# Loading the output weights in 4 KB rows, with selection matmuls, and in DMAs over uneven groups of partitions

## Chip, cores, metric

One core of one Trainium2 chip. The metric is the device time of one execution in microseconds (us); every kernel was run several times and compared with runs of the kernel before on the same chip. Names used below: PE is the matmul engine, PEld its weight loads, DVE, ACT and POOL the vector, scalar and general-purpose engines, and SP the one that issues the large loads; SBUF is the core's memory of 128 partitions, PSUM the one that matmuls write, HBM the chip's main memory. A packet is one entry in the trace's list of what the DMA engines moved, and a load has landed when the last of its completions is in the trace. The profile's span is 1 to 3 us shorter than the device time of the same kernel.

## The reference, cut to what matters

```python
B, Sq, D = 32, 1, 512
Hq, Hkv, Sk, Dh = 32, 8, 2048, 128          # all bfloat16
W = 512                                     # the last 512 rows of the caches are used
q = (x @ wq) -> [B, Hq, 1, Dh]
p = softmax(q . k[:, :, -W:] * Dh**-0.5)    # k, v: [B, Hkv, Sk, Dh], each shared by 4 heads
o = p . v[:, :, -W:]                        # [B, Hq, 1, Dh]
out = o.reshape(B, Sq, Hq*Dh) @ wo          # wo: [4096, 512], 4.19 MB
```

The 512 rows of K and V for 32 batches and 8 heads are 67 MB of the 75.5 MB that are read from HBM, so this is a kernel that streams: its time goes into moving bytes (403 to 411 GB/s while K and V come in).

## The kernel before

One queue (SP) issues every large load: wq, then K and V for the 32 batches, then wo into the place of wq. K and V rows are 4 KB each, 128 partitions a DMA, 512 KB a DMA. wo comes last, in four DMAs whose pieces are 1 KB (one row of wo, 512 numbers): partition d gets row `h*128 + d` for each head h.

```python
WO_CUT = (0, 10, 20, 28, 32)
...
w_sb = sb("w_sb", [P, DKT * HD], BF16)
wo_sb = w_sb[:, :].rearrange("p (h n) -> p h n", h=HQ)
oT_sb = sb("oT_sb", [P, B, HQ], BF16)
...                                          # SP queue, after all K and V issues
sp.wait_ge(pe_qt, 1)
for c in range(4):
    h0, h1 = WO_CUT[c], WO_CUT[c + 1]
    sp.dma_start(
        wo_sb[:, h0:h1, :],
        wo[h0 * DH:h1 * DH, :].rearrange("(h d) n -> d h n", d=P),
    ).then_inc(sem_wo[c], 16)
...                                          # PE, after the last P.V
for hq in range(HQ):
    if hq in WO_CUT:
        pe.wait_ge(sem_wo[WO_CUT.index(hq)], 16)
    for c in range(4):
        ins = pe.matmul(
            KT_ps[:, 0, :].bitcast(F32)[32 * c:32 * (c + 1), 0:128],
            lhsT=oT_sb[:, :, hq], rhs=wo_sb[:, hq, c * 128:(c + 1) * 128],
            start=(hq == 0), stop=(hq == HQ - 1), tile_position=(0, 32 * c),
        )
```

## Time and profile before

| | before |
|---|---|
| time, median of 4 | 198.11 us (197.87 to 198.22) |
| span of the profiled run | 196.5 us |
| last wo part landed | 192.91 us |
| rate while K and V stream | 403 to 411 GB/s |
| rate from 182 to 188 us (wo) | 340 GB/s |
| mean time of a wo packet (1 KB), 182 to 188 us | 50 ns |

From the page of the kernel before: the row of DMA busy tenths and the row of GB/s (40 slices of the span each), the packet line, the chain that ended last (by engine, then by line: L128 issues K, L136 V, L148 wo), the wo matmuls, and the wo issues (size of one, and median us from issue to landing).

```profile
DMA  5999999999999999999999999999999999999970
GB/s 205 425 417 409 411 405 409 411 409 405 409 409 405 408 407 409 410 407 410 404 409 408 409 409 404 410 406 409 406 408 408 408 409 403 409 404 350 338 253 16
DMA packets 23374, 75.95 MB, mean 386 GB/s; under 512 B 2325, under 2 KB 6453, under 8 KB 22837
...
SPq 52%; DMA 37%; PE 7%; issue 2%; DVE 0%
DMA K_sb<-in_k_cache_dram 32%; SPq L136 25%; SPq L128 18%; SPq L148 8%; DMA w_sb<-in_wo_dram 5%; PE KT_ps L229 4%; PE QO_ps L279 1%; PE S_ps L246 1%; SPq L122 1%; PE KT_ps L301 0%; SPq L110 0%; DVE out_sb L368 0%
...
L301 PE MATMUL KT_ps<-w_sb,oT_sb 128*32 128x128 bf16 x128 | 4.3, 313 | 6.6 <-DMA w_sb<-in_wo_dram 6.6
...
w_sb<-in_wo_dram SPq DMA_DIRECT2D x2, 1280.0 KB, 19.3
w_sb<-in_wo_dram SPq DMA_DIRECT2D x1, 1024.0 KB, 12.7
w_sb<-in_wo_dram SPq DMA_DIRECT2D x1, 512.0 KB, 9.9
```

The engines are busy almost everywhere and the chain is DMA and the issuing of DMAs for 89% of the span: nearly all of its time goes into moving bytes, at 403 to 411 GB/s while K and V stream. Only the last four slices fall, 350, 338, 253, 16 GB/s: that is wo.

The table of stretches shows the same end more finely. Its columns are the stretch, its length, the busy us (and instructions) of PE, weight load, DVE, ACT and POOL, then the granted clock, the DMA share and GB/s.

```profile
core 0: us, PE busy (x) PEld busy (x) DVE busy (x) ACT busy (x) POOL busy (x), PEclk, DMA share, GB/s
170.00:176.00 6.00, 2.65 (x48) 2.50 (x48) 3.64 (x7) 1.32 (x3) 0.00 (x0) 0.66 1.03 406
176.00:182.00 6.00, 3.52 (x109) 3.10 (x108) 0.57 (x3) 1.36 (x2) 0.00 (x0) 0.50 1.02 356
182.00:188.00 6.00, 2.02 (x68) 1.70 (x64) 0.19 (x1) 0.00 (x0) 0.00 (x0) 0.50 1.05 340
188.00:194.00 6.00, 3.02 (x88) 2.27 (x88) 0.29 (x1) 0.00 (x0) 0.00 (x0) 0.50 0.42 140
```

One more reading comes from the semaphore events in the trace. A 128-partition DMA gives sixteen completions in the trace; I read them as one from each of the sixteen DMA engines, which the trace doesn't number. These are the completions of the last wo part of the kernel before, in us, sorted:

```
189.31 189.33 189.38 189.46 189.86 189.89 190.04 190.25 190.83 190.96 191.32 192.25 192.32 192.35 192.56 192.91
```

Some engines end 3.6 us behind others. At 14 us the spread was 0.7 us. It grows in steps of about 1.55 us of one completion at a time, each step beside one of the 21 packets of 16 KB in the queue that the page calls "instruction" (about 1.08 us each). Over the K loads the spread jumps at the first, ninth and seventeenth of these (15.05, 85.38 and 152.98 us): from 0.7 to 1.9, from 2.3 to 3.5 and from 3.9 to 5.0 us, so the steps go round eight of the sixteen. In the K load that begins to land at 149.4 us, eight completions lie 3.2 to 3.9 us behind the first and the others at most 1.2 us.

### The profile page before, as it was taken

How to read it: one execution, taken by the hardware profiler on the slowest of the kernel's cores; microseconds unless marked ns; L12 is line 12 of the kernel's file. 1: busy time of each engine (PE TensorE's matmuls, PEld its weight loads, DVE VectorE, ACT ScalarE, POOL GpSimd, SP SyncE). 2: the span in 40 equal slices, each digit the busy share in tenths (PEclk: the TensorE clock that was granted, in tenths of full speed). 3: DMA queues.
4: the chain of work that ended last, by engine and by line, in shares of the span. 5: the costliest groups of instructions: out<-in, count | busy, mean ns of one | idle time of the engine just before them, and what ended most of it. 6: DMA issues, size and time to landing. Idle time of an engine off the chain costs nothing.

```text
span 196.5 us, 6073 instructions
## 1 busy us (share of the span) xinstructions
PE 142.8 (73%) x2692; PEld 116.4 (59%) x2692; DVE 99.8 (51%) x187; ACT 56.5 (29%) x67; POOL 12.1 (6%) x43
## 2 busy tenths in 40 slices
PE   0448994987787797749786979779997599746423
PEld 0337773875575576637665858656975477535322
DVE  0006789645774479424952695457645647541000
ACT  3002434433262145203342325232432052320000
POOL 8102000000000010000000000000000000000000
PEclk9999999699999799985999797996699759955555
DMA  5999999999999999999999999999999999999970
GB/s 205 425 417 409 411 405 409 411 409 405 409 409 405 408 407 409 410 407 410 404 409 408 409 409 404 410 406 409 406 408 408 408 409 403 409 404 350 338 253 16
DMA packets 23374, 75.95 MB, mean 386 GB/s; under 512 B 2325, under 2 KB 6453, under 8 KB 22837
## 3 DMA queue, kind: packets, MB, share of 16 engines
q1 hardware_dynamic: 23300, 75.54, 97.5%
q8 instruction: 21, 0.34, 0.7%
q10 hardware_dynamic: 48, 0.03, 0.2%
q14 instruction: 5, 0.03, 0.0%
HBM read 75.53 MB, written 0.03 MB: 384 GB/s over the span
## 4 chain that ended last, share of the span: by engine, by line
SPq 52%; DMA 37%; PE 7%; issue 2%; DVE 0%
DMA K_sb<-in_k_cache_dram 32%; SPq L136 25%; SPq L128 18%; SPq L148 8%; DMA w_sb<-in_wo_dram 5%; PE KT_ps L229 4%; PE QO_ps L279 1%; PE S_ps L246 1%; SPq L122 1%; PE KT_ps L301 0%; SPq L110 0%; DVE out_sb L368 0%
## 5 line engine op out<-in xcount | busy, mean ns | idle before, releaser
L229 PE MATMUL KT_ps<-perm,K_sb 128*128 128x128 bf16 x1024 | 76.0, 238 | 20.7 <-DMA K_sb<-in_k_cache_dram 20.5
L324 DVE COPY KT_sb<-KT_ps 128x1024 bf16<-128x1024 bf16 x96 | 63.3, 687 | 54.0 <-PE KT_ps L229 53.7
L229 PEld LDWEIGHTS KT_ps<-perm,K_sb 128*128 128x128 bf16 x1024 | 67.5, 108 | 27.1 <-DMA K_sb<-in_k_cache_dram 26.0
L383 ACT ACTIVATE KT_sb<-KT_ps 128x1024 bf16<-128x1024 bf16 x32 | 32.7, 1023 | 81.8 <-PE KT_ps L229 81.8
L279 PEld LDWEIGHTS QO_ps<-PT_sb,V_sb 128*128 128x128 bf16 x1024 | 28.2, 98 | 17.4 <-issue 12.7
L279 PE MATMUL QO_ps<-PT_sb,V_sb 128*128 128x16 bf16 x1024 | 31.1, 171 | 3.7 <-DMA V_sb<-in_v_cache_dram 1.9
L346 DVE TENSOR_SCALAR P_ex<-P_f,recip 32x512 bf16<-32x512 f32 x32 | 25.3, 792 | 1.1
L246 PE MATMUL S_ps<-KT_sb,QBD 128*32 128x512 bf16 x256 | 21.4, 414 | 0.0
L401 ACT ACTIVATE PT_sb<-PT_ps 128x1024 bf16<-128x1024 bf16 x16 | 15.5, 1020 | 20.4 <-PE PT_ps L261 20.4
L261 PE MATMUL PT_ps<-ident,P_ex 128*128 128x128 bf16 x128 | 11.8, 266 | 9.6 <-DVE P_ex L346 9.6
L261 PEld LDWEIGHTS PT_ps<-ident,P_ex 128*128 128x128 bf16 x128 | 10.1, 122 | 10.7 <-DVE P_ex L346 10.7
L189 POOL COPY QBD<-QT_sb 128x32 bf16<-128x32 bf16 x32 | 7.4, 245 | 117.9 <-PE S_ps L246 108.0
L353 DVE CAST oT_sb<-QO_ps 128x32 bf16<-128x32 f32 x32 | 5.9, 183 | 8.9 <-PE QO_ps L279 8.8
L301 PE MATMUL KT_ps<-w_sb,oT_sb 128*32 128x128 bf16 x128 | 4.3, 313 | 6.6 <-DMA w_sb<-in_wo_dram 6.6
L207 PE MATMUL PT_ps<-xT_sb,w_sb 128*128 128x32 bf16 x128 | 4.1, 188 | 6.2 <-DMA w_sb<-in_wq_dram 6.2
L301 PEld LDWEIGHTS KT_ps<-w_sb,oT_sb 128*32 128x32 bf16 x128 | 3.3, 158 | 7.4 <-DMA w_sb<-in_wo_dram 4.7
L207 PEld LDWEIGHTS PT_ps<-xT_sb,w_sb 128*128 128x128 bf16 x128 | 3.7, 104 | 6.6 <-DMA w_sb<-in_wq_dram 4.6
L330 DVE TENSOR_REDUCE maxv<-S_ps 128x1 f32<-128x512 f32 x8 | 5.5, 691 | 4.0 <-PE S_ps L246 4.0
L391 ACT ACTIVATE P_f<-S_ps,negmax 128x512 f32<-128x512 f32 x8 | 5.5, 687 | 5.4 <-DVE negmax L332 5.4
L246 PEld LDWEIGHTS S_ps<-KT_sb,QBD 128*32 128x32 bf16 x256 | 3.9, 96 | 3.7 <-issue 1.0
L316 DVE CAST QT_sb<-PT_ps 128x512 bf16<-128x512 f32 x1 | 0.7, 691 | 10.0 <-PE PT_ps L207 10.0
L368 DVE CAST out_sb<-KT_ps 128x128 bf16<-128x128 f32 x1 | 0.3, 292 | 10.7 <-PE KT_ps L301 10.7
(20 smaller groups left out, 11.9 us busy)
## 6 DMA issues: line engine op xcount, KB each, us to landing
K_sb<-in_k_cache_dram SPq DMA_DIRECT2D x64, 512.0 KB, 15.6
V_sb<-in_v_cache_dram SPq DMA_DIRECT2D x64, 512.0 KB, 15.4
w_sb<-in_wq_dram SPq DMA_DIRECT2D x4, 1024.0 KB, 8.4
w_sb<-in_wo_dram SPq DMA_DIRECT2D x2, 1280.0 KB, 19.3
w_sb<-in_wo_dram SPq DMA_DIRECT2D x1, 1024.0 KB, 12.7
w_sb<-in_wo_dram SPq DMA_DIRECT2D x1, 512.0 KB, 9.9
x_sb<-in_x_dram ACTq DMA_DIRECT2D x1, 32.0 KB, 3.2
out_dram<-out_sb SPq DMA_DIRECT2D x1, 32.0 KB
```

Of the source, the lines that this page charges most:

```text
L128: sp.dma_start(K_sb[:, b % NK, h].rearrange("p r d -> p (r d)"), cache_rows(k_cache, b, h)).then_inc(sem_k[b % NK][h], 16)
L136: sp.dma_start(V_sb[:, b % NV, h].rearrange("p r d -> p (r d)"), cache_rows(v_cache, b, h)).then_inc(sem_v[b % NV], 16)
L148: sp.dma_start(wo_sb[:, h0:h1, :], wo[h0 * DH:h1 * DH, :].rearrange("(h d) n -> d h n", d=P),).then_inc(sem_wo[c], 16)
L207: ins = pe.matmul(PT_ps[:, h // 16, :].bitcast(F32)[:, (h % 16) * 32:(h % 16 + 1) * 32], lhsT=wq_sb[:, kt, h * DH:(h + 1) * DH], rhs=xT_sb ...
L229: ins = pe.matmul(KT_ps[:, t, i * 128:(i + 1) * 128], lhsT=K_sb[:, b % NK, h, 8 * (t % 2) + i, :], rhs=perm[:, :, :], start=True, stop=Tru ...
L246: ins = pe.matmul(S_ps[32 * c:32 * c + 32, :], lhsT=QBD[:, b % NQB, g, :], rhs=KT_sb[:, b % NKT, h, :, c, :], start=(j == 0 and h == 0), s ...
L261: ins = pe.matmul(PT_ps[:, r // 8, (r % 8) * 128:(r % 8 + 1) * 128], lhsT=P_ex[:, r, :, :].rearrange("p s g -> p (s g)"), rhs=ident[:, :], ...
L279: ins = pe.matmul(QO_ps[:, 16 * h:16 * h + 16], lhsT=V_sb[:, b % NV, h, r, :], rhs=PT_sb[:, q % 2, r, :].rearrange("p (c n) -> p c n", c=G ...
L324: dve.tensor_copy(KT_sb[:, b % NKT, t // 2, 8 * (t % 2):8 * (t % 2) + 8, :, :], KT_ps[:, t, :]).then_inc(dve_T, 1)
L346: dve.tensor_scalar(P_ex[rows, :, :, c], P_f32[rows, :].rearrange("p (r s) -> p r s", r=NR), recip[rows, q:q + 1], None, op0=ALU.mult,).th ...
L383: act.activation(KT_sb[:, b % NKT, 1, 8:16, :, :], KT_ps[:, 3, :], ACTF.Copy).then_inc(act_T, 1)
L401: act.activation(PT_sb[:, q % 2, 8 * i:8 * i + 8, :].rearrange("p r n -> p (r n)"), PT_ps[:, i, :], ACTF.Copy,).then_inc(act_PT, 1)
```

## The change

The intent is to shorten the wo phase twice: by 4 KB pieces, and by levelling the sixteen DMA engines. Partition p now gets four neighbouring rows of wo (4 KB in one piece), so the attention output has to be regrouped to match: "selection" matmuls with a band of ones move element d of head h to partition `(h%4)*32 + d//4`, index `d%4`. wo is cut into eight parts of 512 KB, and five of these are issued as DMAs over uneven groups of partitions, which take different numbers of engines.

```diff
-    WO_CUT = (0, 10, 20, 28, 32)
+    NHG = HQ // 4
+    SELCUT = 28
+    WO_SPLIT = [(128,), (4, 4, 120), (56, 72), (40, 88), (2, 6, 120), (24, 104), (128,), (128,)]
@@ SP queue
-            for c in range(4):
-                ...
+            for hg in range(NHG):
+                p0 = 0
+                for m in WO_SPLIT[hg]:
+                    sp.dma_start(
+                        wo_sb[p0:p0 + m, hg].rearrange("p i n -> p (i n)"),
+                        wo[hg * 512 + 4 * p0:hg * 512 + 4 * (p0 + m), :].rearrange("(m i) n -> m (i n)", i=4),
+                    ).then_inc(sem_wo[hg], 16)
+                    p0 += m
@@ PE
+            def select(b0, b1, dst):
+                pe.wait_ge(dve_oT, b1)
+                for i in range(4):
+                    for hi in range(4):
+                        ins = pe.matmul(
+                            dst(i), lhsT=band[:, i, 96 - 32 * hi:224 - 32 * hi],
+                            rhs=oT_sb[:, :, b0:b1].rearrange("p (g hi) b -> p hi g b", hi=4)[:, hi],
+                            start=(hi == 0), stop=(hi == 3), ...)
+                ins.then_inc(pe_sel, 1)
+  ... select(0, 28, ...) after batch 28 of P.V, select(28, 32, ...) at the end
+            for hg in range(NHG):
+                pe.wait_ge(sem_wo[hg], 16 * len(WO_SPLIT[hg]))
+                for i in range(4):
+                    for c in range(4):
+                        ins = pe.matmul(..., lhsT=o_sel[:, i, hg, :], rhs=wo_sb[:, hg, i, c * 128:(c + 1) * 128], ...)
```

Also: DVE and ACT copy the selected output from PSUM, the final result is copied in four pieces by these two engines, and it is stored in 1 KB rows instead of 256 B ones.

More of the change, by code (lines that the diff above doesn't have):

```diff
@@ L52, in bass_standalone__sliding_block_cached__sampling_kernel @@
         wq_sb = w_sb[:, :].rearrange("p (kt n) -> p kt n", kt=DKT)
-        wo_sb = w_sb[:, :].rearrange("p (h n) -> p h n", h=HQ)
+        wo_sb = w_sb[:, :].rearrange("p (g i n) -> p g i n", g=NHG, i=4)
         K_sb = sb("K_sb", [P, NK, 2, NR, DH], BF16)
@@ L61, in bass_standalone__sliding_block_cached__sampling_kernel @@
         PT_sb = sb("PT_sb", [P, 2, NR, P], BF16)
-        oT_sb = sb("oT_sb", [P, B, HQ], BF16)
+        oT_sb = sb("oT_sb", [P, HQ, B], BF16)
+        o_sel = sb("o_sel", [P, 4, NHG, B], BF16)
+        band = sb("band", [P, 4, 224], BF16)
         xT_sb = sb("xT_sb", [P, DKT, 32], BF16)
@@ L66, in bass_standalone__sliding_block_cached__sampling_kernel @@
         x_sb = sb("x_sb", [32, D], BF16)
-        out_sb = sb("out_sb", [P, 128], BF16)
+        out_sb = sb("out_sb", [32, 4, 128], BF16)
         maxv = sb("maxv", [P, NQUAD], F32)
@@ L80, in bass_standalone__sliding_block_cached__sampling_kernel @@
         sem_wq = [sem(f"sem_wq{i}") for i in range(DKT)]
-        sem_wo = [sem(f"sem_wo{i}") for i in range(4)]
+        sem_wo = [sem(f"sem_wo{i}") for i in range(NHG)]
         sem_k = [[sem(f"sem_k{i}_{h}") for h in range(2)] for i in range(NK)]
@@ L91, in bass_standalone__sliding_block_cached__sampling_kernel @@
         pe_fin = sem("pe_fin")
+        pe_sel = sem("pe_sel")
+        dve_sel = sem("dve_sel")
+        act_sel = sem("act_sel")
+        act_out = sem("act_out")
+        pool_band = sem("pool_band")
         pool_perm = sem("pool_perm")
@@ L145, in _ @@
             sp.wait_ge(pe_qt, 1)
-            for c in range(4):
-                h0, h1 = WO_CUT[c], WO_CUT[c + 1]
-                sp.dma_start(
-                    wo_sb[:, h0:h1, :],
-                    wo[h0 * DH:h1 * DH, :].rearrange("(h d) n -> d h n", d=P),
-                ).then_inc(sem_wo[c], 16)
-            sp.wait_ge(dve_out, 1)
+            for hg in range(NHG):
[6 more added lines that the diff above has]
+                    p0 += m
+            sp.wait_ge(dve_out, 2)
+            sp.wait_ge(act_out, 2)
             sp.dma_start(
-                out.rearrange("b s (c n) -> c (b s) n", c=4), out_sb[:, :]
+                out.rearrange("b s n -> b (s n)"), out_sb[:, :, :].rearrange("b c n -> b (c n)")
             ).then_inc(sem_out, 16)
@@ L174, in _ @@
             pool.memset(P_ex[:, :, :, :], 0.0).then_inc(pool_ex, 1)
+            pool.memset(band[:, :, :], 0.0).then_inc(pool_band, 1)
+            pool.wait_ge(pool_band, 1)
+            pool.affine_select(
+                out=band[:, :, :], in_=band[:, :, :], compare_op=ALU.not_equal, fill=1.0,
+                base=384, pattern=[[-1, 4], [-4, 224]], channel_multiplier=1,
+            ).then_inc(pool_band, 1)
             pool.wait_ge(pool_init, 4)
@@ L285, in pv_matmuls @@
                 ins.then_inc(pe_PV, 1)
+            def select(b0, b1, dst):
[3 more added lines that the diff above has]
+                        ins = pe.matmul(
+                            dst(i),
+                            lhsT=band[:, i, 96 - 32 * hi:224 - 32 * hi],
+                            rhs=oT_sb[:, :, b0:b1].rearrange("p (g hi) b -> p hi g b", hi=4)[:, hi],
+                            start=(hi == 0), stop=(hi == 3), tile_position=(0, 0), skip_group_check=True,
+                        )
+                ins.then_inc(pe_sel, 1)
             for it in range(B + PVLAG):
@@ L295, in _ @@
                     pt_transposes((it - 5) // 4)
-            pe.wait_ge(dve_oT, B)
-            for hq in range(HQ):
-                if hq in WO_CUT:
-                    pe.wait_ge(sem_wo[WO_CUT.index(hq)], 16)
-                for c in range(4):
-                    ins = pe.matmul(
-                        KT_ps[:, 0, :].bitcast(F32)[32 * c:32 * (c + 1), 0:128],
-                        lhsT=oT_sb[:, :, hq],
-                        rhs=wo_sb[:, hq, c * 128:(c + 1) * 128],
-                        start=(hq == 0), stop=(hq == HQ - 1), tile_position=(0, 32 * c),
-                    )
+                if it == SELCUT + PVLAG:
+                    pe.wait_ge(pool_band, 2)
+                    pe.wait_ge(dve_T, 3 * B)
+                    pe.wait_ge(act_T, B)
+                    nb = SELCUT
+                    select(0, nb, lambda i: KT_ps[:, i // 2, :].bitcast(F32)[
+                        :, (i % 2) * NHG * nb:(i % 2 + 1) * NHG * nb])
+            nl = B - SELCUT
+            select(SELCUT, B, lambda i: KT_ps[:, 3, :].bitcast(F32)[:, i * NHG * nl:(i + 1) * NHG * nl])
+            pe.wait_ge(dve_sel, 2)
+            pe.wait_ge(act_sel, 1)
+            for hg in range(NHG):
+                pe.wait_ge(sem_wo[hg], 16 * len(WO_SPLIT[hg]))
+                for i in range(4):
+                    for c in range(4):
+                        ins = pe.matmul(
+                            KT_ps[:, 2, :].bitcast(F32)[32 * c:32 * (c + 1), 0:128],
+                            lhsT=o_sel[:, i, hg, :],
+                            rhs=wo_sb[:, hg, i, c * 128:(c + 1) * 128],
+                            start=(hg == 0 and i == 0), stop=(hg == NHG - 1 and i == 3),
+                            tile_position=(0, 32 * c),
+                        )
             ins.then_inc(pe_fin, 1)
@@ L349, in softmax_b, with sel_evac @@
                     ).then_inc(dve_P, 1)
+            def sel_evac(bank, i0, ni, b0, b1):
+                return (
+                    o_sel[:, i0:i0 + ni, :, b0:b1],
+                    KT_ps[:, bank, :].bitcast(F32)[:, 0:ni * NHG * (b1 - b0)].rearrange(
+                        "p (i g b) -> p i g b", i=ni, g=NHG),
+                )
             def ot_evac(b):
                 dve.wait_ge(pe_PV, b + 1)
-                dve.tensor_copy(oT_sb[:, b, :], QO_ps[:, 0:HQ]).then_inc(dve_oT, 1)
+                dve.tensor_copy(oT_sb[:, :, b], QO_ps[:, 0:HQ]).then_inc(dve_oT, 1)
             for it in range(B + PVLAG + 1):
@@ L359, in _ @@
                     ot_evac(it - PVLAG - 1)
+                if it == SELCUT + PVLAG + 1:
+                    dve.wait_ge(pe_sel, 1)
+                    dve.tensor_copy(*sel_evac(0, 0, 2, 0, SELCUT)).then_inc(dve_sel, 1)
                 if it % 4 == 1 and 5 <= it <= B + 1:
@@ L366, in _ @@
                     softmax_a((it - 4) // 4)
+            dve.wait_ge(pe_sel, 2)
+            dve.tensor_copy(*sel_evac(3, 0, 4, SELCUT, B)).then_inc(dve_sel, 1)
             dve.wait_ge(pe_fin, 1)
-            dve.tensor_copy(out_sb[:, :], KT_ps[:, 0, :].bitcast(F32)[:, 0:128]).then_inc(dve_out, 1)
+            for c in range(2):
+                dve.tensor_copy(
+                    out_sb[:, c, :], KT_ps[32 * c:32 * (c + 1), 2, :].bitcast(F32)[:, 0:128]
+                ).then_inc(dve_out, 1)
         @block.scalar
@@ L412, in _ @@
                     pt_evac((it - 5) // 4)
+            act.wait_ge(pe_sel, 1)
+            act.activation(
+                o_sel[:, 2:4, :, 0:SELCUT],
+                KT_ps[:, 1, :].bitcast(F32)[:, 0:2 * NHG * SELCUT].rearrange("p (i g b) -> p i g b", i=2, g=NHG),
+                ACTF.Copy,
+            ).then_inc(act_sel, 1)
+            act.wait_ge(pe_fin, 1)
+            for c in range(2, 4):
+                act.activation(
+                    out_sb[:, c, :], KT_ps[32 * c:32 * (c + 1), 2, :].bitcast(F32)[:, 0:128], ACTF.Copy
+                ).then_inc(act_out, 1)
 _INS = ['x', 'k_cache', 'v_cache', 'wq', 'wo']
```

## The prediction

> **What bounds the kernel now.** The DMA engines. The page shows the 16 engines busy in nearly every slice at 403 to 411 GB/s, PE at 73%, DVE at 51%. The chain that ended last is DMA and DMA issue for 89% of the span. One piece is slower: while wo (4.19 MB in 1 KB rows) arrives, 180 to 190 us, the table of stretches shows 327 to 329 GB/s, and after 189.6 us the DMA share falls from 1.0 through 0.4 to 0.1 before the last landing at 192.9 us. PE is then waiting for wo (6.6 us in four waits) and the end follows the last landing by 3.6 us: 16 matmuls 0.65, copy 0.29, issue 0.69, landing of the output.
>
> Why the falling tail: each DMA's sixteen completions are in the trace. They spread 0.7 us at 14 us, 5.4 us on the last V load, 3.6 us on the last wo part (189.3 to 192.9, mean 190.8). The spread grows in steps of about 1.55 us, one completion at a time, each step beside one of the 16 KB instruction fetches (about 1.08 us each, 21 of them), in a cycle over eight engines. [...] So eight engines end 3.2 to 5.4 us behind.
>
> **What the change does.**
> 1. wo in 4 KB rows. A 4 KB packet took 161 ns; the fastest engine needed about 51 ns per 1 KB row, the slowest about 44. So 64 rows take 10.3 us an engine against 11.3 on the slowest: about 1 us off the end.
> 2. Uneven groups. [...] Perfect levelling would end at about 189.0 us (estimate); I expect 190.5 to 192. No run yet shows which engines lag[...].
> 3. Selection matmuls: 16 with 224 columns before V's batch 29 (about 3 us at the granted 0.5, estimated from 118 ns per 128-column transpose there) and 16 with 32 columns (0.8 us), two copies of 0.3 to 0.7 us. PV then ends near 185 instead of 182.8 us and the wo matmuls (32 ns each, 4.2 us) could end at 190.8 if never waiting. So PE comes to the edge of the critical path and hides below the DMA.
> 4. Output: four small copies on two engines (about +0.2 us), 1 KB output rows instead of 256 B (about -0.4).
> 5. Fourteen issues instead of four, at 0.6 to 1.1 us, fit while the queue is 15 us deep. Early band setup on POOL is hidden.
>
> **Sum.** Last landing 192.9 to about 191.0; tail 3.6 to 3.4. About 2 us less: 196.0 us, eight in ten between 194.4 and 198.2. Faster by over 2%: 0.10; within 2%: 0.87; slower: 0.03.
>
> **Signs.** GB/s near 400 until about 188; completions of the last wo part spread under 3 us; packets of 1 KB nearly gone; PE's wait for wo shorter.
>
> **What would make it wrong.** The lagging engines are the lower ones; the issues stall the queue; the selection matmuls or their evacuation delay PE past the data[...].

The sum came to 196.0 us (194.4 to 198.2): the last landing from 192.9 to about 191.0, of which about 1 us is for the 4 KB rows and the rest, about 1 us, for the groups; and the tail from 3.6 to 3.4 us. The record doesn't say where its 189.0 comes from; the mean of the completions, 190.8 us, less what 64 rows at 161 ns (10.3 us) save against 256 of 1 KB at 44 to 51 ns (about 12.2 us), comes close to it.

## The result, and the profile after

| | before | after |
|---|---|---|
| time, median | 198.11 us (4 runs) | 206.97 us (206.5 to 207.99, 4 runs) |
| ratio to before | | 1.0456, 95% interval 1.0416 to 1.0496 |
| span of the profiled run | 196.5 us | 204.6 us |
| last wo part landed | 192.91 us | 201.36 us |
| from there to the end of the span | 3.6 us | 3.3 us |
| 1 KB or 4 KB wo packet, mean, 182 to 188 us | 50 ns a KB | 285 ns for 4 KB (71 ns a KB) |

A ratio is the mean time of one kernel's fast runs over that of the other's of the same rounds, so not quite the ratio of the medians. The change is 4.6% slower. The same lines of the page after (here L137 issues K, L145 V, L158 wo). In the chain the landing of wo has grown from 5% to 12%:

```profile
DMA  6999999999999999999999999999999999999950
GB/s 215 428 411 408 409 407 408 409 408 411 405 404 408 408 410 408 406 411 407 408 408 409 408 406 411 408 406 410 406 412 402 409 407 408 359 231 212 166 161 22
DMA packets 20320, 75.97 MB, mean 371 GB/s; under 512 B 2310, under 2 KB 2374, under 8 KB 19782
...
SPq 52%; DMA 35%; PE 9%; issue 2%; DVEq 0%; DVE 0%
SPq L145 27%; DMA K_sb<-in_k_cache_dram 23%; SPq L137 20%; DMA w_sb<-in_wo_dram 12%; PE KT_ps L247 6%; SPq L158 5%; PE S_ps L264 2%; PE QO_ps L297 1%; SPq L131 1%; PE KT_ps L341 0%; SPq L119 0%; DVEq L48 0%; DVE out_sb L422 0%
...
L341 PE MATMUL KT_ps<-w_sb,o_sel 128*32 128x128 bf16 x128 | 4.9, 307 | 10.2 <-DMA w_sb<-in_wo_dram 9.8
...
w_sb<-in_wo_dram SPq DMA_DIRECT2D x3, 512.0 KB, 23.5
```

And its table of stretches:

```profile
core 0: us, PE busy (x) PEld busy (x) DVE busy (x) ACT busy (x) POOL busy (x), PEclk, DMA share, GB/s
170.00:176.00 6.00, 2.85 (x48) 2.56 (x48) 3.71 (x7) 1.33 (x3) 0.00 (x0) 0.58 1.03 408
176.00:182.00 6.00, 4.76 (x81) 4.15 (x80) 0.92 (x2) 1.76 (x3) 0.00 (x0) 0.57 1.03 278
182.00:188.00 6.00, 3.41 (x100) 2.70 (x96) 1.18 (x4) 0.00 (x0) 0.00 (x0) 0.72 0.98 223
188.00:194.00 6.00, 1.24 (x32) 0.70 (x32) 0.00 (x0) 0.00 (x0) 0.00 (x0) 0.50 0.95 171
```

Until 176 us nothing differs. Then the rate drops to 278, 223 and 171 GB/s while the DMA share stays at 0.95 to 1.03: the engines are not idle, each packet takes longer. A 4 KB packet takes 161 ns (median) in the K and V stream, and 285 ns in the mean when it belongs to wo. PE's wait for wo grows from 6.6 to 9.8 us (the last number of the matmul line). The 1 KB packets are nearly gone ("under 2 KB" falls from 6453 to 2374), as intended. The completions of the last part are now spread over 17.6 us (183.74 to 201.36), where the prediction wanted under 3.

So the question is why a 4 KB packet of wo is slower than a 4 KB packet of K.

- **Theory A**: the partitions it is written to. Whether a DMA is slow would depend on which of the 128 partitions it writes. The prediction didn't look at this. No trace here shows which engine writes which partition, so the ranges for Theory A are estimates.
- **Theory B**: unequal loads, or the DMAs on fewer than 16 engines. In the trace of the kernel after, the five uneven parts have 23, 26, 21, 23 and 25 completions from 3, 2, 2, 3 and 2 DMAs. If the engines share each DMA's partitions evenly, one for each completion, these totals can be split in one way only (10 and 11 for 40 and 88 partitions), and an engine gets at least 24 and at most 76 of the 4 KB rows, where even parts give 64 (estimate).
- **Theory C**: 4 KB rows of wo are slow to read, or the selection matmuls cost it.
- **Theory D**: 15 issues instead of four.
- **Theory E** (named later): which rows of HBM one DMA reads.

### The profile page after: what moved, and what is told of

The parts are those of the page before. It is cut to its first block, busy times and chain, and to the rows that moved or that the text cites. A ratio compares the mean times of both kernels' runs of the same rounds, so it can differ in the third digit from the quotient of the medians.

```text
span 204.6 us, 6160 instructions
## 1 busy us (share of the span) xinstructions
PE 144.4 (71%) x2724; PEld 116.3 (57%) x2724; DVE 101.9 (50%) x190; ACT 57.6 (28%) x70; POOL 14.8 (7%) x45
## 2 busy tenths in 40 slices
DMA packets 20320, 75.97 MB, mean 371 GB/s; under 512 B 2310, under 2 KB 2374, under 8 KB 19782
## 4 chain that ended last, share of the span: by engine, by line
SPq 52%; DMA 35%; PE 9%; issue 2%; DVEq 0%; DVE 0%
SPq L145 27%; DMA K_sb<-in_k_cache_dram 23%; SPq L137 20%; DMA w_sb<-in_wo_dram 12%; PE KT_ps L247 6%; SPq L158 5%; PE S_ps L264 2%; PE QO_ps L297 1%; SPq L131 1%; PE KT_ps L341 0%; SPq L119 0%; DVEq L48 0%; DVE out_sb L422 0%
## 5 line engine op out<-in xcount | busy, mean ns | idle before, releaser
L247 PE MATMUL KT_ps<-perm,K_sb 128*128 128x128 bf16 x1024 | 74.0, 234 | 24.1 <-DMA K_sb<-in_k_cache_dram 24.0
L247 PEld LDWEIGHTS KT_ps<-perm,K_sb 128*128 128x128 bf16 x1024 | 65.7, 106 | 30.6 <-DMA K_sb<-in_k_cache_dram 28.3
L279 PE MATMUL PT_ps<-ident,P_ex 128*128 128x128 bf16 x128 | 11.1, 255 | 8.8 <-DVE P_ex L387 8.8
L207 POOL COPY QBD<-QT_sb 128x32 bf16<-128x32 bf16 x32 | 8.4, 274 | 114.6 <-PE S_ps L264 106.9
L279 PEld LDWEIGHTS PT_ps<-ident,P_ex 128*128 128x128 bf16 x128 | 9.4, 116 | 9.8 <-DVE P_ex L387 9.7
L401 DVE CAST oT_sb<-QO_ps 128x32 bf16<-128x32 f32 x32 | 9.2, 289 | 7.4 <-PE QO_ps L297 7.4
L341 PE MATMUL KT_ps<-w_sb,o_sel 128*32 128x128 bf16 x128 | 4.9, 307 | 10.2 <-DMA w_sb<-in_wo_dram 9.8
L341 PEld LDWEIGHTS KT_ps<-w_sb,o_sel 128*32 128x32 bf16 x128 | 2.8, 128 | 12.1 <-DMA w_sb<-in_wo_dram 11.7
L422 DVE CAST out_sb<-KT_ps 32x128 bf16<-32x128 f32 x2 | 0.6, 280 | 14.9 <-PE KT_ps L341 14.8
L477 ACT ACTIVATE out_sb<-KT_ps 32x128 bf16<-32x128 f32 x2 | 0.5, 270 | 20.2 <-PE KT_ps L341 20.2
## 6 DMA issues: line engine op xcount, KB each, us to landing
K_sb<-in_k_cache_dram SPq DMA_DIRECT2D x64, 512.0 KB, 15.6
V_sb<-in_v_cache_dram SPq DMA_DIRECT2D x64, 512.0 KB, 15.4
```

The lines of the kernel that those rows point to most:

```text
L247: ins = pe.matmul(KT_ps[:, t, i * 128:(i + 1) * 128], lhsT=K_sb[:, b % NK, h, 8 * (t % 2) + i, :], rhs=perm[:, :, :], start=True, stop=Tru ...
L279: ins = pe.matmul(PT_ps[:, r // 8, (r % 8) * 128:(r % 8 + 1) * 128], lhsT=P_ex[:, r, :, :].rearrange("p s g -> p (s g)"), rhs=ident[:, :], ...
L401: dve.tensor_copy(oT_sb[:, :, b], QO_ps[:, 0:HQ]).then_inc(dve_oT, 1)
```

## The experiments

Sixteen kernels ran. In all of them the last wo landing and the packet times are read from the trace; "packet" means the mean time of a 4 KB packet between 182 and 188 us. Both come from the one profiled run of a kernel; for w1_120 and z4_level that was the fastest of its runs. The runs were made in batches on three chips, and the kernel before had medians of 198.02 to 198.38 us in them, so kernels of different batches are best compared by their ratios.

| run | time, median us | ratio to before, 95% interval | last wo landing, us | packet, ns |
|---|---|---|---|---|
| before | 198.11 | | 192.91 | (50 for 1 KB) |
| after | 206.97 | 1.0456 (1.0416 to 1.0496) | 201.36 | 285 |
| x1_even | 196.44 | 0.9920 (0.9894 to 0.9946) | 191.30 | 162 |
| x2_halves | 203.74 | 1.0261 (1.0209 to 1.0314) | 198.61 | 290 |
| x3_stride2 | 196.37 | 0.9908 (0.9892 to 0.9924) | 191.32 | 162 |
| x4_before_uneven | 208.52 | 1.0537 (1.0507 to 1.0566) | 202.90 | (87 for 1 KB) |
| y1_one_group | 200.00 | 1.0111 (1.0083 to 1.0138) | 194.82 | 254 |
| y3_stride_src | 202.77 | 1.0240 (1.0220 to 1.0261) | 197.63 | 269 |
| y4_stride_dest | 196.63 | 0.9930 (0.9910 to 0.9950) | 191.60 | 162 |
| z3_middle | 202.57 | 1.0210 (1.0188 to 1.0232) | 197.30 | 253 |
| w1_120 | 199.95 | 1.0085 (1.0056 to 1.0114) | 194.14 | 247 |
| z1_early_select | 196.58 | 0.9912 (0.9896 to 0.9928) | 191.51 | 163 |
| z2_level | 198.58 | 1.0018 (0.9999 to 1.0036) | 193.41 | 193 |
| m64_at0 | 209.84 | 1.0574 (1.0549 to 1.0599) | 205.22 | 322 |
| m64_at16 | 208.04 | 1.0484 (1.0465 to 1.0503) | 203.11 | 313 |
| m64_at32 | 196.90 | 0.9922 (0.9902 to 0.9942) | 191.55 | 162 |
| z4_level | 199.50 | 1.0056 (1.0022 to 1.0090) | 193.28 | 265 |

The sixteenth, the probe p1_probe, had one look and no rounds (197.45 us, state unknown as for any single run; only its completions are used).

### x1_even: undo the uneven groups alone

```diff
-    WO_SPLIT = [(128,), (4, 4, 120), (56, 72), (40, 88), (2, 6, 120), (24, 104), (128,), (128,)]
+    WO_SPLIT = [(128,)] * 8
```

> The changed kernel with all eight wo parts issued as one DMA over 128 partitions; everything else of the change kept. Theory A[...]: 4 KB wo packets back at 159 to 170 ns, last wo landing about 192 us, time 195.5 to 198 us. Theory B[...]: also about 196. Theory C (4 KB rows of wo are slow to read from HBM, or the selection matmuls cost it): stays at 205 to 208.

Measured 196.44 us, last landing 191.30 us, packets 162 ns. Its stretches:

```profile
176.00:182.00 6.00, 4.76 (x60) 4.00 (x58) 0.30 (x1) 1.94 (x2) 0.00 (x0) 0.50 1.03 410
182.00:188.00 6.00, 4.44 (x140) 3.99 (x141) 1.81 (x5) 0.54 (x1) 0.00 (x0) 0.78 0.89 354
188.00:194.00 6.00, 3.07 (x116) 2.57 (x108) 0.56 (x2) 0.54 (x2) 0.00 (x0) 0.78 0.19 72
```

410 GB/s right through the start of wo, where the kernel after had 278. (354 and 72 GB/s later are because engines finish, see the falling share.) Theory C is out: rows, selection and tail are all still in this kernel, and it is 0.8% faster than before. The whole loss comes from the one line with the groups.

### x2_halves and x3_stride2: equal loads, different partitions

```diff
-    WO_SPLIT = [(128,), (4, 4, 120), ...]
+    WO_SPLIT = [(64, 64)] * 8                       # x2_halves
```
```diff
+                rows = wo[hg * 512:(hg + 1) * 512, :].rearrange("(m two i) n -> two m (i n)", two=2, i=4)
+                for t in range(2):                  # x3_stride2: partitions t, t+2, t+4, ...
+                    dst = bass.AP(tensor=w_sb, offset=t * DKT * HD + hg * 2048, ap=[[2 * DKT * HD, 64], [1, 2048]])
+                    sp.dma_start(dst, rows[t]).then_inc(sem_wo[hg], 16)
```

> All eight wo parts as two DMAs of 64 neighbouring partitions[...]. Theory A:[...] packets over 220 ns while both halves are not mixed, last landing 197 to 203 us, time 201 to 208. Theory B: [...]as x1_even, 195.5 to 198. Theory D (number of issues): 16 issues as against 14, so as slow as the changed kernel, 205 to 208.

> All eight wo parts as two DMAs of 64 partitions, every second one: [...]16 issues[...]. Theory A: between x1_even and x2_halves, last landing 193 to 197, time 197 to 201. Theory B: as x1_even. Theory D: as slow as the changed kernel and as x2_halves.

In both, every DMA has sixteen completions, so four rows for each engine if they are shared evenly (estimate). x2_halves took 203.74 us with packets of 290 ns, x3_stride2 196.37 us with 162 ns. These are the stretches of x2_halves:

```profile
176.00:182.00 6.00, 4.76 (x77) 4.01 (x76) 0.81 (x2) 1.89 (x3) 0.00 (x0) 0.50 1.05 251
182.00:188.00 6.00, 2.96 (x91) 2.58 (x88) 1.25 (x5) 0.03 (x1) 0.00 (x0) 0.78 1.03 228
188.00:194.00 6.00, 2.47 (x64) 1.40 (x64) 0.04 (x1) 0.00 (x0) 0.00 (x0) 0.50 0.93 259
```

and two of x3_stride2:

```profile
176.00:182.00 6.00, 4.76 (x78) 4.04 (x77) 0.84 (x2) 1.88 (x3) 0.00 (x0) 0.50 1.03 410
182.00:188.00 6.00, 4.44 (x158) 4.06 (x159) 1.26 (x5) 0.00 (x0) 0.00 (x0) 0.78 0.89 354
```

DMAs of sixteen completions each are slow as well, so fewer than 16 engines or unequal loads are not needed for the loss (against B), and sixteen issues can be fast (against D). I had expected x3_stride2 to lose a little (197 to 201 us); it lost nothing.

### x4_before_uneven: uneven groups in the kernel before

```diff
-                sp.dma_start(wo_sb[:, h0:h1, :], wo[...].rearrange("(h d) n -> d h n", d=P)).then_inc(sem_wo[c], 16)
+                rows = wo[h0 * DH:h1 * DH, :].rearrange("(h d) n -> d h n", d=P)
+                for p0, p1 in ((0, 56), (56, 128)):
+                    sp.dma_start(wo_sb[p0:p1, h0:h1, :], rows[p0:p1]).then_inc(sem_wo[c], 16)
  ... PE waits for 32 instead of 16
```

> The kernel before, in its 1 KB rows and without selection, but each of its four wo DMAs split into partitions 0-55 and 56-127[...]. Theories A and B: slower than before by 4 to 10 us (202 to 208). Theory C: no change, about 198.

208.52 us, a little past the expected 202 to 208. Packets of 1 KB took 87 ns instead of 50. So the loss doesn't need the 4 KB rows: it goes with the groups.

### y1_one_group and w1_120: one uneven part alone

```diff
+    WO_SPLIT = [(128,)] * 3 + [(40, 88)] + [(128,)] * 4        # y1_one_group
+    WO_SPLIT = [(128,)] * 3 + [(4, 4, 120)] + [(128,)] * 4     # w1_120
```

> x1_even with only the fourth part uneven (40 and 88 partitions[...]). Theory A[...]: about a fifth to a third of the loss, last landing 1.5 to 4 us later than x1_even, time 197.5 to 200.5. If the loss needed many small DMAs[...]: within 1 us of x1_even.

> x1_even with only the second part uneven, as in the change: 4, 4 and 120 partitions[...]. [...] Theory A[...]: last landing 1 to 4 us after x1_even's 191.3, time 197.4 to 200.5. [...]

(The expectation of w1_120 speaks of the second part; the edit makes the fourth part uneven, as in y1_one_group.) One part of eight with 40 and 88 partitions moves the last landing by 3.5 us (191.30 to 194.82), one with 4, 4 and 120 by 2.8 us (to 194.14). Five such parts in the kernel after cost 10.1 us. In both kernels the even parts suffer too while the uneven one is in flight: in y1_one_group its completions run from 180.76 to 189.95 us, of the packets that start from 182 to 183 us none takes under 260 ns, and from 189 us on the mean is back at 166 ns or less. These two have unequal loads besides. Counted as under Theory B (21 completions as 10 and 11, 23 as 4, 4 and 15), the fullest engines have at most 68 rows instead of 64 in y1_one_group and 66 in w1_120; at 162 ns a row that is 0.65 and 0.32 us (estimate), so the loads alone don't explain 3.5 and 2.8. In the kernel after it would be at most 12 rows, 1.9 us, of the 10.1 (estimate).

### y3_stride_src and y4_stride_dest: source or destination

x2_halves and x3_stride2 differ in the rows they read too. Both kernels here give a wrong result: y3_stride_src writes halves but reads every second row, y4_stride_dest writes every second partition but reads 256 KB in one piece.

```diff
-  wo[hg * 512 + 4 * p0:...].rearrange("(m i) n -> m (i n)", i=4)             # in x2_halves
+  rows = wo[...].rearrange("(m two i) n -> two m (i n)", two=2, i=4)          # y3_stride_src
-  .rearrange("(m two i) n -> two m (i n)", two=2, i=4)                        # in x3_stride2
+  .rearrange("(two m i) n -> two m (i n)", two=2, i=4)                        # y4_stride_dest
```

> Wrong result on purpose. Destination as x2_halves (64 neighbouring partitions a DMA), source as x3_stride2 (every second 4 KB row of wo). Theory A (which partitions are written decides): slow as x2_halves, 201 to 205. Theory E (which HBM rows are read decides): fast, 196 to 197.

> Wrong result on purpose. Destination as x3_stride2 (every second partition), source as x2_halves (256 KB in one piece a DMA). Theory A: fast as x3_stride2, 196 to 197. Theory E: slow, 201 to 205.

202.77 and 196.63 us: the time follows the destination. Theory E is out.

### z3_middle: a first test of the place, nearly undecided

```diff
+    WO_SPLIT = [(32, 64, 32)] * 8
```

> All eight wo parts as three DMAs over partitions 0-31, 32-95 and 96-127 ([...]more DMAs than x2_halves). [...]between x1_even and x2_halves, last landing 193.5 to 197 us, time 198.5 to 202, faster than x2_halves (203.7) in spite of more and smaller DMAs. If any range of fewer than 128 neighbouring partitions is slow: as x2_halves or worse, 203.5 or more.

202.57 us, last landing 197.30 us: just outside the expected 198.5 to 202 (the landing is just outside too). It is faster than x2_halves by 1.2 us in the median, in spite of more DMAs, and its packets fell from 290 to 253 ns, which is near a half-and-half mean of 162 and 322 ns (242; 322 is m64_at0's, below). But the two ran on different chips, and the intervals of their ratios overlap.

### m64_at0, m64_at16, m64_at32: only the start partition differs

All of wo goes in sixteen DMAs of 64 neighbouring partitions that always start at the same partition (half of the columns goes into K's buffer, idle by then). The result is wrong; bytes, sources, sizes and counts are those of x2_halves. The queue also waits once, for K's last transposes, in all three; wo's issues still begin at 167.1 to 167.6 us.

```diff
+            sp.wait_ge(pe_T[3], B)
+            ...                                  # k_flat: K_sb as [P, columns]
+            for hg in range(NHG):
+                for t in range(2):
+                    dst = (w_sb[:, :], k_flat)[t][START:START + 64, hg * 2048:(hg + 1) * 2048]   # 0, 16 or 32
+                    sp.dma_start(dst, wo[hg * 512 + 256 * t:hg * 512 + 256 * (t + 1), :]...).then_inc(sem_wo[hg], 16)
```

> Wrong result on purpose. All of wo in 16 DMAs of 64 partitions, always partitions 0-63 (half of the columns into K's idle buffer); source, size and count as x2_halves. [...]packets about 300 to 325 ns, last landing 197 to 201 us. If a narrow range alone is slow: the same.

> Wrong result on purpose. As m64_at0, partitions 16-79: [...]two kinds of packets, about 160 and about 320 ns, and the last part's 16 completions in two groups of 8, one at 186 to 191 us, one at 196 to 202. If a narrow range alone is slow: one kind of packet, as m64_at0.

> Wrong result on purpose. As m64_at0, partitions 32-95: [...] Packets back at 160 to 165 ns, last landing 191 to 192.5 us. If a narrow range alone is slow: as m64_at0, 197 to 201.

The stretches of 176 to 182 and 182 to 188 us, for the start at partition 0:

```profile
176.00:182.00 6.00, 4.76 (x79) 4.09 (x79) 0.90 (x2) 1.83 (x3) 0.00 (x0) 0.50 1.05 235
182.00:188.00 6.00, 2.84 (x88) 2.49 (x85) 1.21 (x5) 0.00 (x0) 0.00 (x0) 0.50 1.03 207
```

for the start at 16:

```profile
176.00:182.00 6.00, 4.82 (x80) 4.16 (x80) 0.92 (x2) 1.66 (x3) 0.00 (x0) 0.56 1.05 222
182.00:188.00 6.00, 1.87 (x64) 1.80 (x64) 0.59 (x2) 0.00 (x0) 0.00 (x0) 0.72 1.03 212
```

and for the start at 32:

```profile
176.00:182.00 6.00, 4.76 (x59) 3.96 (x57) 0.30 (x1) 1.94 (x2) 0.00 (x0) 0.50 1.03 412
182.00:188.00 6.00, 4.44 (x146) 4.03 (x148) 1.81 (x5) 0.54 (x1) 0.00 (x0) 0.78 0.90 358
```

In the second stretch the first engines of the start at 32 are done from 185.7 us on (share 0.90), so these rates don't compare like with like. From 184 to 186 us the engines are busy in both kernels (share 1.01 and 1.03); first the start at 0, then the start at 32:

```profile
184.00:186.00 2.00, 0.53 (x20) 0.56 (x21) 0.00 (x0) 0.00 (x0) 0.00 (x0) 0.50 1.01 205
184.00:186.00 2.00, 1.43 (x51) 1.25 (x47) 0.43 (x2) 0.00 (x0) 0.00 (x0) 0.89 1.03 410
```

Partitions 0 to 63: 205 GB/s and packets of 322 ns; 32 to 95: 410 GB/s and 162 ns. A shift of the start by 32 doubles the rate. So a narrow range alone is not slow: its place decides. The last landing of the start at 0, 205.22 us, is later than the 197 to 201 I expected; the packets were as expected. The start at 16 failed my expectation: its last landing, 203.11 us, is just past the late group's 196 to 202, and there are not two kinds of packets. Nearly all of its packets between 182 and 188 us took about as long as each other (288 of 306 between 290 and 340 ns), and its last part's completions are not two groups. Why the starts at 0 and 16 are slow and the start at 32 is not, no trace shows: the trace doesn't tell which engine writes which partition, so this stays open.

### p1_probe: which engines run behind

```diff
+            for j, m in enumerate((4, 8, 12)):
+                sp.dma_start(probe[0:m, j, :], wo[0:m, 0:64]).then_inc(sem_probe[j], 16)
```

> x1_even with three tiny DMAs over 4, 8 and 12 partitions put in the queue between the last V load and wo, each with its own semaphore[...]. If the engines that lag are the upper eight (what the prediction assumed), the 8 completions of the second all lie within 2.3 us of its first, and the last four of the third lie 3 us or more behind. If it is the lower eight, the 8 completions are all among the late ones of the loads around them, 3 to 5.4 us behind the first completion of the last V load. If neither, they are mixed. Time as x1_even.

The events on the three semaphores (the first of each comes 8 us or more before the others and is not counted as a completion):

```
 4 partitions: 167.93 | 176.45 176.78 177.30 178.43
 8 partitions: 168.29 | 176.60 176.63 176.97 177.05 177.48 178.62 179.52 179.70
12 partitions: 168.64 | 176.81 176.82 176.84 177.14 177.25 177.66 178.80 179.73 179.91 181.28 181.46 181.48
```

4, 8 and 12 completions for 4, 8 and 12 partitions (and in the kernel after 21 completions and two early events for 40 and 88 partitions). Of the four none is more than 2.0 us behind the first of its DMA; of the eight two are, by 2.9 and 3.1 us; of the twelve five, by 2.9 to 4.7 us. So the completions of the second are neither all early nor all late, but mixed. Which engines these are the trace doesn't show. So whether the lagging engines were the ones that the groups meant to spare was not shown.

### z1_early_select, z2_level, z4_level: is there more to gain?

z1_early_select puts the first selection two batches earlier, where PE waits anyway:

```diff
-    SELCUT = 28
+    SELCUT = 26
-                if it == SELCUT + PVLAG + 1:        # DVE's copy of it
+                if it == SELCUT + PVLAG + 2:
```

> x1_even with the first selection over 26 batches, two batches earlier, in a stretch where PE waits anyway. If the selection is off the critical path in x1_even, as its trace says (PE waits for the last wo part there): within 0.4 us of x1_even's 196.4. If it holds up the end: 1 to 2 us faster.

196.58 us, the same as x1_even's 196.44. PE's first wo matmul moved from 187.47 to 184.18 us and nothing came of it: the selection is off the critical path once wo is even.

z2_level and z4_level are meant to hand out rows unevenly over engines again, but through every fourth partition: 21 DMAs for one part, and 8 DMAs for four parts. How many rows each engine got the trace doesn't show.

```diff
+            ...                                      # z2_level: the first three parts, even; then
+            wo_part(LAST, 0, 0, 32)                  # 32 partitions in one DMA,
+            for b4 in range(4): wo_part(LAST, 1, 8 * b4, 8)      # 32 in DMAs of 8,
+            for t in (2, 3):
+                for b8 in range(8): wo_part(LAST, t, 4 * b8, 4)  # 64 in DMAs of 4
+            ...                                      # the other four parts, even
```
```diff
+            for t in range(3): wo_part(t, 0, 32)     # z4_level: the same idea, four parts in each DMA
+            for b4 in range(3): wo_part(3, 8 * b4, 8)
+            for b8 in range(2): wo_part(3, 24 + 4 * b8, 4)
+            ...                                      # the other four parts, even
```

> z1_early_select with the last wo part handed out unevenly over engines[...]: every fourth partition[...]. If unequal loads are harmless[...]: last landing 190.3 to 191 us, time 195.4 to 196.4. If unequal loads or 21 more issues hurt by themselves: slower than z1_early_select by 1 us or more.

> z1_early_select with the first four wo parts together handed out unevenly over engines in only 8 DMAs of every fourth partition[...]. z2_level failed at its aim because its 21 issues took 14.5 us. If unequal loads are harmless[...]: last landing 190.2 to 191 us, time 195.4 to 196.2, faster than z1_early_select. [...]

Neither helped: 198.58 and 199.50 us. In z2_level the queue itself became the limit, as its timeline shows (start, length, engine, line, count):

```profile
170.48 14.46 SPq L161 DMA_DIRECT2D w_sb<-in_wo_dram  x21
184.99 1.86 SPq L164 DMA_DIRECT2D w_sb<-in_wo_dram  x4
```

21 issues took 14.46 us, 0.69 each (the sets of 4 and 6 neighbouring partitions in the kernel after took 0.26 to 0.39), so the last four parts were issued only from 185 us on. z4_level issued in time, and its packets rose to 265 ns. Why was not shown. z4_level's six runs also scatter from 198.14 to 200.57 us. Whether engines can be levelled at all in this way stays open. Perfect levelling would have something to give: the sixteen completions of x1_even's last part run from 186.41 to 191.30 us with a mean of 188.74, 2.6 us before the last (estimate).

The best kernels are x1_even and x3_stride2, 0.8 to 0.9% faster than before and 5% faster than the change.

## Why the prediction was wrong

It gave 196.0 us (194.4 to 198.2) and 0.87 for "within 2%". Measured: 206.97 us.

1. **4 KB rows: right.** Predicted 64 rows in 10.3 us an engine, about 1 us off the end. In x1_even, which has this and no uneven groups, packets took 162 ns and the last landing moved by 1.6 us, from 192.91 to 191.30 (its parts are smaller too, eight instead of four; that was not separated).
2. **Uneven groups: this is the step that failed.** The prediction said "Perfect levelling would end at about 189.0 us (estimate); I expect 190.5 to 192", by counting rows for each engine at 161 ns a row. The last landing was at 201.36 us. The time of a row was taken as fixed. It isn't: a 4 KB packet took 285 ns, because of the partitions that each DMA writes. x1_even (remove the groups: fast), x2_halves and x3_stride2 (sixteen completions a DMA in both: slow or fast by the partitions alone), y3_stride_src and y4_stride_dest (destination, not source) and m64_at0 against m64_at32 (start partition alone: 205 against 410 GB/s) show it. Why these partitions and not others was not shown. The term was worth about 1 us of gain in the sum and cost 10.1 us (191.30 to 201.36). The premise about which engines lag was not shown either; with a predicted gain of 1 us at stake, that is a small matter beside 10.
3. **Selection matmuls: right.** Predicted about 3 us and 0.8 us, "hides below the DMA"; they took 3.15 and, in x1_even, 0.58 us. z1_early_select shows that they don't count.
4. **Tail: about right.** Predicted 3.4 us from the last landing to the end of the span; 3.3 after, 3.1 in x1_even. The issue of the output's store fell from 0.69 to 0.35 us in the kernel after; the copies, two on each engine, took 0.56 and 0.59 us instead of one of 0.29.
5. **Issues: right in effect.** They were 15, not fourteen as I had written, and ran from 167.1 to 177.3 us, with the data landing long after (19.3 to 24.0 us from issue to landing for the three whole parts; 15.4 and 15.6 us, median, for V and K). The band was set up by 7.5 us and first used at 178.1 us.
6. **Signs.** "GB/s near 400 until about 188", "spread under 3 us" and "PE's wait for wo shorter" (6.6 to 9.8 us) came out false; the first two pointed at the step that failed. With the groups undone the time is 196.44 us, 0.4 from the sum of 196.0, but that is partly luck: the sum counts about 1 us for the groups, and the rows alone moved the landing by 1.6 instead of 1.

None of the things listed under "what would make it wrong" was the cause. The list looked at engines, queue and PE; it didn't ask where the bytes land.

## What to carry to other kernels

A DMA's speed depended on the partitions it writes as well as on its row length (50 ns for 1 KB before, 162 for 4 KB in x1_even): keep 128 partitions in one DMA. Of the narrower sets tried alone, every second partition and the 64 from 32 on ran at full rate (162 ns); the 64 from 0 and from 16 on did not (322 and 313 ns). What decides this was not shown, so for other sets it has to be measured. If you split a load by partitions to steer or level engines, compare the packet times with those of an ordinary load first. And read GB/s and packet times beside the DMA busy row: in the slow stretch the engines looked 95% busy or more at about half the rate (223 and 171 GB/s after 182 us, against 408 before 176 us).
